# A state-space block and feed-forward on one core: kernel units multiplied by twos, shift added behind the move, gate row spread by DMA, another order

## The chip, the cores and the metric

The kernel runs on one core of one Trainium2 chip. The core has five engines that run beside each other and wait for one another by semaphores: TensorE (PE in the profile, with its weight loads shown as PEld), VectorE (DVE), ScalarE (ACT), GpSimd (POOL) and SyncE (SP), which here issues nearly all DMAs. The metric is the device time of one execution in microseconds; lower is better.

## The reference

All numbers are float32, the sequence has L = 2048 positions, the width is D = 512, the state has N = 128 entries per channel, and the feed-forward is F = 1792 wide.

```
mod = silu(c) @ w_mod                      # six rows of 512: sa, ca, ga, sb, cb, gb
h = layernorm(x) * (1 + ca) + sa
K[d, l] = Re sum_n C[d,n] * exp(dt[d] * A[d,n] * l) * dt[d] * B[d,n]
y = causal convolution of h with K along l  (the reference does it by FFT of length 2 L)
x = x + ga * (y + h * Dskip)
h = layernorm(x) * (1 + cb) + sb
x = x + gb * (relu(h @ w1 + b1)**2 @ w2 + b2)
```

## The kernel before

The convolution is a hand-made transform of the rows in two steps: `stage1` (L784) and `stage2` (L793), each made of small TensorE products, for the input (`u_pieces`, eight blocks c of 64 channels, letters A to H) and for the convolution kernel K. A product in frequency (`product_pieces`, letters a to h: L949 on DVE, then L957 on PE, L963 on DVE) and the inverse (`inverse`, L1131) follow. Then the second normalization and the feed-forward (from L1245 on, some 280 us, mostly products by split float32r parts).

The head (`row_pieces`, L727 to 748) takes the 16 rows of the input, 128 positions by 512 channels each. For every row DVE subtracts the mean and multiplies by a gain row (L729), ACT makes a scaled selection matrix (L737), and PE moves the row into another layout: first a product `pick` x `shift` (L739), which opens the accumulation with the additive part (the shift row s4, made from the modulation group S), and then 32 small products (L742) that add to it. ACT copies the sum from PSUM to `xj` (L745). The gain row needs the modulation groups G and C, the shift needs S as well. Modulation groups are products of PE with 1 MB slabs of `w_mod` (L698).

The string `LOADS` gives the order of the first loads on SP: p and P are the two halves of the state's parameters, x a row of the input, G, C, S the slabs, t the 2 MB table of `stage2`, k and e small tables.

The convolution kernel K is generated in 32 units of 16 channels. For a unit u POOL adds phases (`kgen_phase`, L892) and multiplies amplitudes (`kgen_amp`, L914 and L918) into one of three buffers (`amps[u % 3]`); ACT makes sine and cosine (L902 to 904) into PSUM; DVE multiplies both (`kgen_rl`, L928 to 931); PE multiplies the unit's two halves with each other (`kgen_mm`, L938: 32 products of 32 columns, 64 records since float32 takes two passes) into one half of the bank `kg`; ACT copies it, DVE adds the skip weight (L1018, L1019), and `stage1` takes it on. `finish(u)` (L1010) does all that from the product on.

The string `ORDER` says, for each unit, which other pieces stand behind it in the program (r rows, x exponentials, p parameters, letters for blocks, w loads of w1, l late modulation). That order gives the buffers and the dependencies. The order on each engine is then made by `keep_order` (L181), a list scheduler with its own costs (`weight`, L121): it runs the program forward and backward in turns (`PASSES`), and neighbouring PE instructions that write the same tensor stay together as one group. SP takes what is ready in the order of the program. Instructions named in `in_turn` keep their relative order on PE. Loads after the head go through `paced_load` (L668), at most two in flight.

Around the change of phase, the gate row gb (L762, four rows of 32 equal copies in `gb4`) is spread over all partitions into `gbb` by four products with a broadcast column of the identity and an ACT copy (L1067 to 1071). `gbb` lies in the tile `lo`, which the phases use up to the last unit. The first two calls of `inverse` (rows 0 to 3) add the untouched input, loaded again into `cs_` by the loop at L1089, and their products are put into `in_turn`.

## Time and profile before

| | us |
|---|---|
| median of three runs | 605.31 |
| lowest and highest of them | 601.77, 606.57 |
| profiled execution, its own time | 605.23 |
| span of the profiled execution | 603.4 |

| engine | busy us | share of the span | instructions |
|---|---|---|---|
| PE | 569.5 | 94% | 9396 |
| PEld | 494.1 | 82% | 9396 |
| DVE | 438.4 | 73% | 714 |
| ACT | 421.5 | 70% | 788 |
| POOL | 464.0 | 77% | 383 |

The page gives a profile of one execution. A row of a timeline has start and duration in us, the engine, the line of the code, the operation, the tiles written and read, the shape and how many instructions were merged, and in brackets how long the engine stood idle before it and what ended that wait. Shares are means over stages with different limits, so each part of the change has to be read in its own stage.

### The profile page before, as it was taken

How to read it: one execution, taken by the hardware profiler on the slowest of the kernel's cores; microseconds unless marked ns; L12 is line 12 of the kernel's file. 1: busy time of each engine (PE TensorE's matmuls, PEld its weight loads, DVE VectorE, ACT ScalarE, POOL GpSimd, SP SyncE). 2: the span in 40 equal slices, each digit the busy share in tenths (PEclk: the TensorE clock that was granted, in tenths of full speed). 3: DMA queues.
4: the chain of work that ended last, by engine and by line, in shares of the span. 5: the costliest groups of instructions: out<-in, count | busy, mean ns of one | idle time of the engine just before them, and what ended most of it. 6: DMA issues, size and time to landing. Idle time of an engine off the chain costs nothing.

```text
span 603.4 us, 21634 instructions
## 1 busy us (share of the span) xinstructions
PE 569.5 (94%) x9396; PEld 494.1 (82%) x9396; DVE 438.4 (73%) x714; ACT 421.5 (70%) x788; POOL 464.0 (77%) x383
## 2 busy tenths in 40 slices
PE   1898999999999999998989999999999999998996
PEld 1667988999999998997778888888887888887885
DVE  7796688899798799746888945459859744547833
ACT  4997999998999879442879555546957555654440
POOL 5599999999999799160668998926689688892544
PEclk9999999999999999998999999999999999999999
DMA  8962033302130234274351332015354343201432
GB/s 306 398 193 72 5 73 74 64 12 44 34 74 4 51 104 100 52 195 145 103 147 57 105 104 89 22 45 176 107 153 127 112 119 102 70 18 35 158 88 86
DMA packets 45982, 60.70 MB, mean 101 GB/s; under 512 B 5184, under 2 KB 26816, under 8 KB 45760
## 3 DMA queue, kind: packets, MB, share of 16 engines
q1 hardware_dynamic: 45456, 59.20, 33.5%
q8 instruction: 73, 1.20, 0.9%
q10 hardware_dynamic: 432, 0.14, 0.1%
q14 instruction: 21, 0.17, 0.1%
HBM read 46.74 MB, written 4.19 MB: 84 GB/s over the span
## 4 chain that ended last, share of the span: by engine, by line
PE 69%; ACT 8%; POOL 7%; DVE 6%; issue 5%; DMA 4%; DVEq 0%; POOLq 0%; ACTq 0%; SPq 0%
PE ac L1245 9%; PE ps L1245 8%; PE ps L957 8%; PE ps L799 8%; PE ps L789 6%; PE ac L1274 4%; PE ac L1272 4%; PE ac L1273 4%; PE kg L938 4%; DMA xy<-w 4%; PE kg L1245 3%; PE ac L1131 3%; PE ps L1274 2%; PE ps L1272 2%; PE ps L1273 2%
## 5 line engine op out<-in xcount | busy, mean ns | idle before, releaser
L1214 POOL TENSOR_TENSOR w2r<-xy,w2r 128x512 fp32r<-128x512 f32 x56 | 80.1, 1431 | 53.9 <-ACT w2r L1213 53.7
L799 PE MATMUL ps<-xy,t_sb 128*64 128x64 f32 x2048 | 67.3, 223 | 1.0 <-issue 0.7
L799 PEld LDWEIGHTS ps<-xy,t_sb 128*64 128x64 f32 x2048 | 64.2, 138 | 3.1 <-issue 0.9
L957 PE MATMUL ps<-e_sb,xy 128*64 128x128 f32 (+2 forms) x1152 | 65.3, 267 | 1.1 <-issue 0.8
L957 PEld LDWEIGHTS ps<-e_sb,xy 128*64 128x64 f32 x1152 | 59.5, 140 | 2.6 <-issue 1.4
L1213 ACT CAST w2r<-xy 128x512 fp32r<-128x512 f32 x56 | 34.8, 624 | 27.1 <-PE ac L1274 12.7
L918 POOL TENSOR_TENSOR rtl<-tables 128x1024 f32<-128x1024 f32 x22 | 43.2, 1964 | 0.0
L1272 PE MATMUL ac<-w2r,r 128*128 128x512 f32 x110 | 42.8, 389 | 0.0
L1273 PE MATMUL ac<-w2r,r 128*128 128x512 f32 x110 | 42.8, 389 | 0.0
L1274 PE MATMUL ac<-w2r,r 128*128 128x512 f32 x110 | 42.8, 389 | 0.0
L791 ACT COPY xy<-ps 128x512 f32<-128x512 f32 x64 | 36.6, 590 | 8.7 <-PE ps L789 8.4
L1245 PE MATMUL ac<-tt,k1t 128*128 128x512 f32 x168 | 40.6, 390 | 1.5 <-DVE xy L1378 1.5
L949 DVE TENSOR_TENSOR xy<-ps,xy 128x512 f32<-128x512 f32 x64 | 40.1, 685 | 2.1 <-PE ps L799 1.1
L1245 PEld LDWEIGHTS ac<-tt,k1t 128*128 128x128 f32 x168 | 31.5, 188 | 8.4 <-DVE xy L1378 1.9
L1145 POOL TENSOR_TENSOR big<-big,xy 128x512 f32<-128x512 f32 x12 | 16.1, 1357 | 26.3 <-ACT big L1142 26.2
L1237 POOL TENSOR_TENSOR k1t<-xy,k1t 128x1024 fp32r<-128x1024 f32 x14 | 33.7, 2407 | 3.3 <-ACT k1t L1235 3.1
L892 POOL TENSOR_TENSOR rtl<-lo,big 128x1024 int32<-128x1024 int32 x16 | 34.3, 2143 | 2.4 <-ACT tg L904 2.3
L963 DVE COPY big<-ps 128x256 f32<-128x256 f32 (+1 forms) x66 | 24.7, 411 | 15.7 <-PE ps L957 15.5
L892 POOL TENSOR_TENSOR llph<-lo,big 128x1024 int32<-128x1024 int32 x16 | 34.5, 2157 | 0.8 <-ACT tg L904 0.8
L1272 PE MATMUL ps<-w2r,r 128*128 128x512 f32 (+1 forms) x88 | 34.7, 394 | 0.0
L789 PE MATMUL ps<-d_sb,big 128*64 128x128 f32 x512 | 32.1, 274 | 2.4 <-ACT xy L791 1.7
L1274 PE MATMUL ps<-w2r,r 128*128 128x512 f32 (+1 forms) x88 | 34.0, 386 | 0.0
(297 smaller groups left out, 1693.8 us busy)
## 6 DMA issues: line engine op xcount, KB each, us to landing
xy<-w SPq DMA_DIRECT2D x91, 256.0 KB, 2.8
xy<-xt SPq DMA_DIRECT2D x32, 256.0 KB, 4.5
xy<-xy SPq DMA_DIRECT2D x32, 256.0 KB, 3.6
xy<-w_mod SPq DMA_DIRECT2D x6, 1024.0 KB, 9.0
out_dram<-p SPq DMA_DIRECT2D x15, 256.0 KB, 2.0
t_sb<-c_t SPq DMA_DIRECT2D x1, 2048.0 KB, 11.5
i2c<-c_i SPq DMA_DIRECT2D x4, 512.0 KB, 4.2
big<-prm SPq DMA_DIRECT2D x2, 768.0 KB, 6.2
```

The source lines that it names most:

```text
L789: nc.tensor.matmul(ps[64 * r : 64 * r + 64, 128 * i : 128 * i + 128], src[:, i], d1_sb[:, r], start=True, stop=True)
L791: copy(dst[:, o // 4], ps.rearrange("p (t m) -> p m t", t=4))
L799: nc.tensor.matmul(ps[64 * r : 64 * r + 64, 64 * i : 64 * i + 64].rearrange("p (h q t) -> p q h t", h=2, t=2), t2_sb[:, 8 * g + i, r], src ...
L892: nc.gpsimd.tensor_tensor(ph.rearrange("p d r (a b) -> p (d r) a b", a=4), bc(low_phase[:, us].rearrange("p d r b -> p (d r) b"), 2, 4), b ...
L918: nc.gpsimd.tensor_mul(am[:, 0, :, 32:96].rearrange("p d (v x) -> p d v x", v=2), bc(et[:, 256 + 8 * d0 : 384 + 8 * d0].rearrange("p (y a) ...
L949: nc.vector.tensor_mul(product_piece(y, g), ps, piece(x, g))
L957: nc.tensor.matmul(ps[64 * m : 64 * m + 64], pairs(y)[:, g, i // 2, 64 * m : 64 * m + 64, i % 2], e1_sb[:, h].rearrange("p (r j) -> p r j" ...
L1214: nc.gpsimd.tensor_sub(to[:, 1], wst, to[:, 0].bitcast(F32))
L1245: nc.tensor.matmul(ps[:, cols], x, y, start=(i == 0 and not onto), stop=(i == 5), skip_group_check=onto)
L1272: pe.append(nc.tensor.matmul(bank_, r2l[:, ms], hi_[:, cols], start=(f == begin), stop=False))
L1273: pe.append(nc.tensor.matmul(bank_, r2h[:, ms], lo_[:, cols], start=False, stop=False))
L1274: pe.append(nc.tensor.matmul(bank_, r2h[:, ms], hi_[:, cols], start=False, stop=(f == end_)))
```

## The change

1. `PAIRS`: the products of two neighbouring units are issued one behind the other (`finish_pair`), and the rest of both units follows. One pair of the 16, units 8 and 9, stays apart.
2. `EVAC`: nine of the 16 rows (g, v) have no product with `pick`. For v (five rows) DVE adds the shift while it moves the row out of PSUM, in place of ACT's copy; for g (four rows) ACT copies as before and POOL adds the shift in place. The seven rows a stay as they were.
3. The gate row is spread by 16 DMAs on SP, from 32 partitions to 32 partitions of 128 numbers each, in place of four products and a copy.
4. Four input rows are loaded into `p1` by a piece y, behind the last unit's amplitudes, and the first inverse adds these; the later rows use `ds_` alone.
5. The products of the first two inverse calls are no longer held in their turn on PE.
6. `LOADS`, `ORDER`, `PASSES` (7 to 11) and the scheduler's cost of a transpose are changed, and so the order on every engine.

```
-LOADS = "pxxxxxxxxGCSxxxxxxxkPtxe"
+PAIRS = "1111011111111111"
+EVAC = "gggvaaaaagavvavv"
+LOADS = "xxxpxxxGCxexPSxtxxxxkxxx"
...
-PASSES, SPAN = 7, 400
+PASSES, SPAN = 11, 400
...
 ORDER = (
-    "rrrrrrrrrrxxrrrrrrBCCBpACCBCBAABCCBAB.AAAAC..lB.0aaaa1.a.Daa.x.DabbbbDEDEE.b.2Ebb.bD.DcDccccEDc.E.Fc"
-    "3EFc.E.ddddGd.Fd.GxFd4.F.dGeeeeF..FGGFHeGeGe5..wHeffGHfff.w.f.H.HffH6ggHgw.g.g.H.g7ghhhghw"
+    "rrrrrrrrrrrrrrrrCBCCBAxAAACBlBCCBxAC.p.AACBA.0.BBaaaa1..aDaDa.D.abbbbEE.Db..bEE2bD.bDDcEccDc3..EccxE"
+    ".cFE.cFddFddGdFddF.4.d..eeFee..GGGGFF5xe..eeGeffHwHfGfGfHHfw..H..6HHffggHgg...g.ygw7hwhhhgg"
...
+            if ins.is_transpose:
+                return 88, 88 + 130
...
-            nc.tensor.matmul(ps.rearrange("p (g d) -> p g d", g=4), pick, bc(shift, 1, 4), start=True, stop=False)
+            late = EVAC[s] != "a"
+            if not late:
+                nc.tensor.matmul(ps.rearrange("p (g d) -> p g d", g=4), pick, bc(shift, 1, 4), start=True, stop=False)
...
-                        row[:, 128 * q : 128 * q + 128], start=False, stop=(g == 3))
-            moved.append(nc.scalar.copy(xj[:, :, 4 * s : 4 * s + 4], ps.rearrange("p (g d) -> p d g", g=4)))
+                        row[:, 128 * q : 128 * q + 128], start=late, stop=late or g == 3)
+            to, of = xj[:, :, 4 * s : 4 * s + 4], ps.rearrange("p (g d) -> p d g", g=4)
+            if EVAC[s] == "v":
+                nc.vector.tensor_add(to, of, bc(s4, 2, 4))
+            else:
+                nc.scalar.copy(to, of)
+            if EVAC[s] == "g":
+                nc.gpsimd.tensor_add(to, to, bc(s4, 2, 4))
...
+    def finish_pair(u):
+        if u % 2:
+            for x in (u - 1, u):
+                if x in kq:
+                    kgen_mm(kq.pop(x), kg[:, x % 2])
+            for x in (u - 1, u):
+                if x > finished[-1]:
+                    finish(x)
+        elif PAIRS[u // 2] == "0":
+            kgen_mm(kq.pop(u), kg[:, 0])
+            finish(u)
...
-        kgen_mm(kq.pop(u), kps)
...
+    def early_rows():
+        assert amped[-1] == NU - 1
+        late.append(held(kp, "k01", "p1", [P, 7, 512]))
+        for s in range(4):
+            paced_load(late[0][:, 3 + s], xt[s])
+        yield
...
-            finish(u - 1)
+            finish_pair(u - 1)
...
-    gps = bank("ps", PS)
     for q in range(4):
-        nc.tensor.matmul(
-            gps[:, 128 * q : 128 * q + 128], ident[:, 32 * q : 32 * q + 1].to_broadcast([P, P]), gb4, start=True, stop=True)
-    nc.scalar.copy(gbb, gps)
+        for k in range(4):
+            nc.sync.dma_start(
+                gbb[32 * k : 32 * k + 32, 128 * q : 128 * q + 128], gb4[32 * q : 32 * q + 32])
...
-    xts = [cs_[s] if s < 4 else ds_[s % 4] for s in range(16)]
-    for s in range(8):
+    xts = [ds_[s % 4] for s in range(16)]
+    for s in range(4, 8):
         paced_load(xts[s], xt[s])
...
-    cd4 = runs(spectra[3]).rearrange("p (s q c d) -> p s q c d", s=4, q=4, c=NC)
+    cd4 = p1[:, 3:7].rearrange("p s (q c d) -> p s q c d", q=4, c=NC)
...
-        if s0 < 4:
-            in_turn.update(whole)
```

More of the change, by code (lines that the diff above doesn't have):

```diff
@@ L743, in row_pieces @@
                         ps[32 * q : 32 * q + 32, 128 * g : 128 * g + 128], sel[:, g // 2, 32 * (g % 2) : 32 * (g % 2) + 32],
-                        row[:, 128 * q : 128 * q + 128], start=False, stop=(g == 3))
-            moved.append(nc.scalar.copy(xj[:, :, 4 * s : 4 * s + 4], ps.rearrange("p (g d) -> p d g", g=4)))
+                        row[:, 128 * q : 128 * q + 128], start=late, stop=late or g == 3)
[6 more added lines that the diff above has]
+                nc.gpsimd.tensor_add(to, to, bc(s4, 2, 4))
+            moved.append(s)
             if s % 4 == 3:
@@ L1032, in load_pieces @@
             yield
-    work["w"] = load_pieces()
+    late = []
+    def early_rows():
[4 more added lines that the diff above has]
+        yield
+    work["w"], work["y"] = load_pieces(), early_rows()
     next(work["x"])
@@ L1094, in tile_adaln_ssm_ffn @@
     w2r = held(kp, "k00", "w2r", [P, 3, 2, 512], FR)
-    p1 = held(kp, "k01", "p1", [P, 7, 512])
+    p1 = late[0]
     for _ in last:
```

## The prediction

> **What bounds the kernel now.** I read the page's parts first, then busy times by stage, then the timeline of each engine in the first 56 us, then the waits of POOL, and last single products in the middle.
>
> ```profile
> core 0: us, PE busy (x) PEld busy (x) DVE busy (x) ACT busy (x) POOL busy (x), PEclk, DMA share, GB/s
> 0.00:24.60 24.60, 9.86 (x112) 7.98 (x112) 17.14 (x61) 16.11 (x68) 15.43 (x32) 1.00 0.92 336
> 24.60:49.00 24.40, 23.22 (x528) 16.01 (x528) 23.80 (x48) 23.16 (x65) 19.31 (x26) 1.00 0.62 217
> 49.00:265.00 216.00, 209.97 (x6084) 199.77 (x6086) 177.58 (x290) 188.96 (x293) 196.29 (x144) 1.00 0.26 59
> 320.00:603.40 283.40, 276.93 (x1240) 228.63 (x1238) 179.34 (x217) 161.19 (x279) 209.83 (x167) 1.00 0.31 93
> ```
>
> The rows are stretches of the span, each with the busy time of every engine. Until 24.6 us PE works 9.86 us, because parameters and modulation weights are still arriving. The row stage (24.6 to 49) has PE, DVE and ACT all above 23 of 24.4 us: three engines bind at once. From 49 to 265 PE is busy 210 of 216 us and POOL 196. After 320 PE is busy 277 of 283 us and the diff touches nothing that it does there, so whatever is saved ahead of 320 should come through whole.
>
> **Row stage.** Its start and its pace on PE:
>
> ```profile
> xy<-xt SPq DMA_DIRECT2D x32, 256.0 KB, 4.5
> xy<-w_mod SPq DMA_DIRECT2D x6, 1024.0 KB, 9.0
> big<-prm SPq DMA_DIRECT2D x2, 768.0 KB, 6.2
> 20.38 1.93 PE L698 MATMUL ps<-xy,srep 128*32 128x128 f32 x32 [0.86 <-DMA xy<-w_mod]
> 26.08 1.08 PE L742 MATMUL ps<-xy,big 128*32 128x128 f32 x32 [0.98 <-DVE xy L729]
> 27.09 0.49 PE L739 MATMUL ps<-shift,pick 128*128 128x512 f32 x1
> 27.52 1.08 PE L742 MATMUL ps<-xy,big 128*32 128x128 f32 x32
> 37.86 2.72 DVE L729 SCALAR_TENSOR_TENSOR xy<-xy,mv,kg 128x512 f32<-128x512 f32 x4
> 49.51 2.84 PE L789 MATMUL ps<-d_sb,big 128*64 128x128 f32 x48 [0.70 <-ACT big L745]
> L745 ACT COPY big<-ps 128x512 f32<-128x512 f32 x16 | 9.3, 587 | 1.1 <-PE ps L742 1.0
> L949 DVE TENSOR_TENSOR xy<-ps,xy 128x512 f32<-128x512 f32 x64 | 40.1, 685 | 2.1 <-PE ps L799 1.1
> L1145 POOL TENSOR_TENSOR big<-big,xy 128x512 f32<-128x512 f32 x12 | 16.1, 1357 | 26.3 <-ACT big L1142 26.2
> POOL big L592 <- DMA big<-prm: 5.5, 1, 5.5
> ```
>
> A shift product takes PE's slot from 27.09 to 27.52, 0.43 us, and the 32 products of a row 1.01. Nine rows lose the shift product: 9 x 0.43 = 3.9 us of PE. The first four rows (g, g, g, v) need it no more, so a row waits for the gate and the scale weights (G and C) alone and no longer for the third group S at 20.38 to 22.3. Six rows instead of eight now lie ahead of G and C: 0.5 MB less, at the 336 GB/s of the first window 1.5 us. S was the 1 MB behind C, 3 us more at that rate. Without both, and with the same steps behind, the first row comes 4.5 us earlier, at about 21.6 instead of 26.08. Four such rows fill PE until 25.6. Row 4 is the first with a shift product, and S now has the second parameter load ahead of it, 0.75 MB or 2.3 us; the first shift product ended the wait at 24.6, so row 4 begins at 26.9, and five rows of 1.01 and seven of 1.44 end at 42.0 instead of 48.6. So for PE alone the stage would end 6.6 us earlier. DVE and ACT don't allow that. ACT loses five copies, 5 x 0.587 = 2.9 us, and was busy 23.16 of 24.4. DVE gains five additions out of PSUM; the nearest row is L949's 0.685, so +3.4 us. The last L729 ended at 40.58; with no earlier start, 3.4 us of additions, a row's products (1.08) and one addition more (0.69) let the next stage (L789) begin at 45.8 instead of 49.5, a gain of 3.7; with DVE's start 4.5 us earlier it would be 8.2. Ends 2.9 (ACT) and 6.6 (PE). I take 4.5, nearer the low end, because ACT and DVE were both full. Four rows get an addition in place on POOL; nearest row L1145 with 1.36, 5.4 us in all. What covers them is POOL's 5.5 us wait for the second parameter load. This load now has eight rows ahead of it instead of 15, and two weight groups instead of three: 2.75 MB less, 8 us at 336 GB/s, so the cover is partly eaten by the very gain; POOL's first unit can still start earlier, or at worst as before. The first parameter load goes behind three rows, 2.2 us; POOL's first product on it (L592) waits for the step sizes of L586 anyway: I take nothing, at most 2.2 lost. Rows 9 to 15 now lie behind the table t, but what lies ahead of the last row is the same set of loads: nothing.
>
> **Products by twos.** PE has to change from 64-column to 32-column tiles and back for each unit (L938):
>
> ```profile
> 67.85 1.10 PE L799 MATMUL ps<-xy,t_sb 128*64 128x64 f32 x32
> 68.78 1.04 PE L789 MATMUL ps<-d_sb,ksb 128*64 128x128 f32 x16
> 69.66 1.10 PE L799 MATMUL ps<-xy,t_sb 128*64 128x64 f32 x32
> 70.69 1.12 PE L938 MATMUL kg<-rtl 128*32 128x64 f32 x64
> 71.74 3.02 PE L799 MATMUL ps<-xy,t_sb 128*64 128x64 f32 x96
> 74.69 1.12 PE L938 MATMUL kg<-llph 128*32 128x64 f32 x64
> 92.16 0.97 PE L938 MATMUL kg<-llph 128*32 128x64 f32 x52
> 93.78 0.43 PE L938 MATMUL kg<-llph 128*32 128x64 f32 x12 [0.65 <-issue]
> ```
>
> Thirty-two L799 take 0.93 us ahead of L789 (67.85 to 68.78) and 1.03 ahead of L938. The 96 behind it take 2.95, 0.16 above three times 0.93, of which 0.10 belongs to the next change: 0.05 for the change back. Inside a unit the broken block gives (0.97 - 0.43) / 40 = 13.5 ns per record, so 64 need 0.86, and the unit took 1.05: another 0.19. A unit costs 0.15 to 0.34 us for its changes, and 15 of the 16 pairs lose one such set: 2.3 to 5.1 us of PE.
>
> Against it stands a wait. There are three amplitude buffers, and POOL (L914) writes unit u+2's into that of u-1. With pairs the product of u-1 waits for DVE's L931 of u, so POOL may go on only some 2.2 us (two units' products) behind the end of that L931:
>
> ```profile
> 77.95 1.21 DVE L931 TENSOR_TENSOR rtl<-rtl,tg 128x1024 f32<-128x1024 f32 x1
> 80.14 1.10 POOL L914 TENSOR_TENSOR llph<-tables 128x512 f32<-128x512 f32 x1
> 206.09 1.21 DVE L931 TENSOR_TENSOR llph<-llph,tg 128x1024 f32<-128x1024 f32 x1
> 202.78 1.07 POOL L914 TENSOR_TENSOR rtl<-tables 128x512 f32<-128x512 f32 x1 [0.83 <-PE kg L938]
> 228.60 1.22 DVE L931 TENSOR_TENSOR rtl<-rtl,tg 128x1024 f32<-128x1024 f32 x1
> 230.15 1.07 POOL L914 TENSOR_TENSOR llph<-tables 128x512 f32<-128x512 f32 x1
> 241.26 1.95 POOL L918 TENSOR_TENSOR rtl<-tables 128x1024 f32<-128x1024 f32 x1
> 254.96 1.12 PE L938 MATMUL kg<-rtl 128*32 128x64 f32 x64
> 240.52 1.03 ACT L902 ACTIVATE tg<-llph 128x1024 f32<-128x1024 int32 x1
> ```
>
> The first two rows are units 3 and 5: POOL began at 80.14 and would have to wait until 79.16 + 2.2 = 81.4, so 1.2 us. In the middle pair it is 6.7, in the last 1.9. Over the 14 pairs kept together that have a unit u+2, five would make POOL wait, together 12.2 us at the dates of before; for the other nine the buffer is free anyway. Behind the waiting L914 on POOL stand L918 and the next phase (L892), and ACT's sines and DVE wait for these. POOL has room: its last amplitude ends at 243.2 and the last unit's product runs at 254.96, 11.8 us later. Three ACT passes like L902's (3.1) and DVE's two long and two short ones (2 x 1.21 and 2 x 0.685, 3.8) take 6.9 of these. So 4.9 us of POOL's delay cost nothing, and the new order can draw DVE's work forward. Net of this I take 3.5 of the 5.1, with ends +5.1 and -7.3 (12.2 less 4.9).
>
> **Gate row.** Removed: four products (eight records) and a copy.
>
> ```profile
> 266.01 1.16 PE L1069 MATMUL ps<-gb,ident 128*128 128x128 f32 x8
> 267.48 5.38 PE L957 MATMUL ps<-e_sb,xy 128*64 128x32 f32 x160 [0.30 <-DVE xy L949]
> 240.29 0.35 SPq L1318 DMA_DIRECT2D lo<-b  x1
> 253.06 4.68 SPq L669 DMA_DIRECT2D xy<-xy  x4
> ```
>
> PE gains 267.18 - 266.01, 1.1 us (nothing, if it then waits for DVE all the same). Sixteen moves of 16 KB come onto SP. Their place is free once the last phase is made, about where the load of b2 is issued, 240.29; an issue takes 0.35, 16 make 5.6 us, and the next thing on SP is the swap at 253.06: 12.8 us of cover. If one cost more than 0.8 us the swap, and with it the last block's products, would be late by the rest. I take nothing.
>
> **Early rows, inverse out of turn, transposes' weight, passes.** Four loads move off the stretch from 270 on. The first sum of the inverse waited there for PE and not for a load: nothing. The freer order of the first inverse can move single waits; bounds -1 to +1.5, I take nothing.
>
> **Sum.** 4.5 + 3.5 + 1.1 = 9.1 us. The profiled execution took 605.23 us (span 603.4 and 1.8 around it), the median of the runs is 605.31, the same within 0.1. So 605.2 - 9.1 = 596.1, say 596.
>
> [...] The group of L698 at 20.38 takes 1.93 us for 32 records:
>
> ```profile
> 78.78 1.95 PE L698 MATMUL ps<-xy,srep 128*32 128x128 f32 x64
> ```
>
> In the middle 64 of them take 1.95: in the head PE runs at half pace, although the row of that window gives a granted clock of 1.00; from L742 at 26.08 on the pace is full. A row stage that begins sooner, behind less work, could begin at the half pace. If its first four rows do, they take 8.1 us instead of 4 and end at 29.7 instead of waiting for 26.9: 2.8 us of the gain are lost, 598.8. I give it a small chance, since DVE feeds a row every 0.69 us and PE should be dense at once. [...]
>
> **Rivals.** (1) All comes out: head 6.6, pairs 5.1, gate 1.1 give 592.4, with the inverse 590.9. For: PE is the bound nearly everywhere. Against: ACT and DVE in the row stage. (2) The waits eat the pairs, or ACT holds the head: head 2.9, pairs 0 to -2, gate 0 to 1.1 give 601 to 604, no change that counts. For: ACT at 23.16 of 24.4. This is also the case in which the edits do not do what they say. (3) Slower: POOL becomes the bound. If the amplitude buffer's wait stays 12.2 us and POOL starts no earlier, because its four additions fill the 5.5 us, its last amplitude ends at 255.4 and the last unit's product at 262.3 instead of 254.96: 7.3 later, 612.5 (the gate's 1.1 being lost in DVE's wait). It decides once POOL's delay passes 4.9 us plus what its start gains. Against: the five waits are mostly a question of the place of DVE's work.
>
> **Chances.** A measurement of this kernel can tell about 1%, 6.05 us, from no change. Forecast 0.47 (own range 592 to 599), slow clock at the start 0.07, all comes out 0.13: faster 0.67. Rival 2 has 0.24, rival 3 has 0.09. The range 590 to 605 leaves out rival 3, a little of rival 2 and little more, 0.15 to 0.2 together.
>
> **What would show it.** The first L742 near 21.6 us and the first L789 near 45; L739 seven times; L938 in blocks of 128; POOL's waits for PE kg under 5 us in the sum; no L1069; SP free again before the last swap. Wrong would be: the first L789 at 48 or later, or POOL's last L918 later than 243.

## The result and the profile after

The changed kernel takes 613.15 us in the median of four runs (612.24 to 614.34), the kernel before 604.65 beside it (601.77 to 606.57): 1.0145 times as long, interval 1.0113 to 1.0176. The forecast was 596.0, range 590 to 605. The profiled execution of the changed kernel took 614.34 us, span 612.5.

Where the time goes can be read from the starts of a few groups on TensorE. Line numbers of the changed kernel lie further down: L653 became L657, L742 L748, L739 L745, L745 L755, L789 L802, L914 and L918 L927 and L931, L938 L951, L1131 L1163, L1272 L1302. The row move of VectorE is L753, GpSimd's row addition L757.

| us from the start of the span | before | after | difference |
|---|---|---|---|
| first product of a row (L742, L748) | 26.08 | 22.60 | -3.5 |
| first product of stage 1 (L789, L802) | 49.51 | 50.00 | +0.5 |
| end of the last unit's products (L938, L951) | 256.08 | 261.60 | +5.5 |
| first product of the inverse (L1131, L1163) | 272.79 | 281.05 | +8.3 |
| first product of the second feed-forward matrix (L1272, L1302) | 320.15 | 328.64 | +8.5 |
| end of the span | 603.4 | 612.5 | +9.1 |

So rows begin sooner, but the stage behind them does not, and then 8 us are lost up to the inverse. The busy times by stretch of after, for the stretches that the prediction showed of before (columns as there, then TensorE's granted clock, DMA share and GB/s):

```profile
24.60:49.00 24.40, 19.64 (x519) 15.06 (x511) 22.61 (x46) 22.79 (x64) 23.93 (x28) 0.98 0.74 252
49.00:265.00 216.00, 202.03 (x5858) 191.18 (x5860) 184.28 (x285) 179.07 (x286) 189.35 (x139) 0.98 0.23 53
```

In the row stage TensorE has 3.6 us less to do than before (19.64 for 23.22) and GpSimd 4.6 more (23.93 for 19.31). From 49 to 265 every engine but VectorE is busy for less time than in before: something makes them stand. Among the groups of VectorE, ScalarE and GpSimd, VectorE's integer shifts are the only one whose longest member jumped, from 0.95 to 7.81 us. The group of that line in before and then in after (shortest, median, longest ns):

```profile
L653 DVE TENSOR_SCALAR big<-big x10: 283/675/951, 14.3 to 120.9; 128x512 int32<-128x512 int32 x6, 128x256 int32<-128x256 int32 x4
```

```profile
L657 DVE TENSOR_SCALAR big<-big x10: 292/802/7814, 12.5 to 137.5; 128x512 int32<-128x512 int32 x6, 128x256 int32<-128x256 int32 x4
```

VectorE's timeline of after around the longest one:

```profile
101.19 1.22 DVE L942 TENSOR_TENSOR llph<-llph,tg 128x1024 f32<-128x1024 f32 x1
102.32 7.81 DVE L657 TENSOR_SCALAR big<-big 128x512 int32<-128x512 int32 x1
110.06 0.67 DVE L943 TENSOR_TENSOR llph<-llph,tg 128x512 f32<-128x512 f32 x1
110.66 0.15 DVE L1042 TENSOR_TENSOR ksb<-kg,ds 128x4 f32<-128x4 f32 x1
...
116.70 0.42 DVE L657 TENSOR_SCALAR big<-big 128x512 int32<-128x512 int32 x1
```

The shift of the same shape at 116.70 takes 0.42 us, this one 7.81. GpSimd's timeline meanwhile:

```profile
101.83 1.07 POOL L927 TENSOR_TENSOR rtl<-tables 128x512 f32<-128x512 f32 x1
102.86 1.96 POOL L931 TENSOR_TENSOR rtl<-tables 128x1024 f32<-128x1024 f32 x1
104.77 2.15 POOL L905 TENSOR_TENSOR rtl<-lo,big 128x1024 int32<-128x1024 int32 x1
106.86 1.08 POOL L927 TENSOR_TENSOR rtl<-tables 128x512 f32<-128x512 f32 x1
107.89 1.97 POOL L931 TENSOR_TENSOR rtl<-tables 128x1024 f32<-128x1024 f32 x1
113.95 2.13 POOL L905 TENSOR_TENSOR llph<-lo,big 128x1024 int32<-128x1024 int32 x1 [4.10 <-ACT tg L917]
```

Five products follow one another without a gap, and the shift ends (110.13) when the fifth does (109.86) and GpSimd has to wait for ScalarE. What stands behind the shift on VectorE is small, but others wait for it. The timelines of ScalarE and of TensorE in after, and the busy times of the stretch behind:

```profile
110.84 0.37 ACT L1041 COPY ksb<-kg 128x256 f32<-128x256 f32 x1 [6.01 <-DVE ksb L1042]
```

```profile
111.52 1.98 PE L802 MATMUL ps<-d_sb,big 128*64 128x128 f32 x16 [5.14 <-DVE big L976]
113.28 3.63 PE L802 MATMUL ps<-d_sb,ksb 128*64 128x128 f32 x32
```

```profile
110.00:130.00 20.00, 18.48 (x426) 17.96 (x428) 17.98 (x32) 16.58 (x28) 12.94 (x10) 0.83 0.23 49
```

ScalarE stands 6.01 us, TensorE 5.14, and then TensorE runs at half pace: 16 of these products take 1.98 us (the prediction's row has 1.04), 32 take 3.63, and the granted clock of the stretch is 0.83. GpSimd then stands 4.10 us too, because the sines that it waits for were late. On TensorE alone that is 5.14 us of standing and, against the pace of the prediction's row, some 2.5 us of half pace ((1.98 - 1.04) + (3.63 - 2.08)), 7.6 in all from one 0.4 us instruction. The experiments had to show whether this is so, and why the change gains nothing even beside it.

### The profile page after: what moved, and what is told of

The parts are those of the page before. It is cut to its first block, busy times and chain, and to the rows that moved or that the text cites. A ratio compares the mean times of both kernels' runs of the same rounds, so it can differ in the third digit from the quotient of the medians.

```text
span 612.5 us, 21636 instructions
## 1 busy us (share of the span) xinstructions
PE 565.7 (92%) x9379; PEld 493.0 (80%) x9379; DVE 450.5 (74%) x719; ACT 415.1 (68%) x780; POOL 467.5 (76%) x387
## 4 chain that ended last, share of the span: by engine, by line
PE 66%; DVE 13%; POOL 10%; ACT 5%; issue 4%; DMA 1%; SPq 0%; DVEq 0%; POOLq 0%; ACTq 0%
PE ac L1275 9%; PE ps L1275 7%; PE ps L970 6%; PE ps L802 5%; PE ps L812 5%; PE ac L1302 4%; PE ac L1303 4%; PE ac L1304 4%; PE ps L1304 3%; PE ps L1303 3%; PE ps L1302 3%; PE kg L1275 3%; DVE xy L962 3%; PE kg L951 2%; PE ac L1163 2%
## 5 line engine op out<-in xcount | busy, mean ns | idle before, releaser
L970 PE MATMUL ps<-e_sb,xy 128*64 128x128 f32 (+2 forms) x1152 | 63.9, 266 | 1.6 <-issue 1.0
L804 ACT COPY xy<-ps 128x512 f32<-128x512 f32 x64 | 36.9, 594 | 11.0 <-PE ps L802 10.9
L931 POOL TENSOR_TENSOR rtl<-tables 128x1024 f32<-128x1024 f32 x22 | 43.3, 1970 | 0.0
L1302 PE MATMUL ac<-w2r,r 128*128 128x512 f32 x110 | 42.8, 389 | 0.0
L962 DVE TENSOR_TENSOR xy<-ps,xy 128x512 f32<-128x512 f32 x64 | 40.0, 685 | 1.7 <-PE ps L812 1.1
L802 PE MATMUL ps<-d_sb,big 128*64 128x128 f32 x512 | 33.2, 280 | 8.5 <-DVE big L976 5.1
L802 PEld LDWEIGHTS ps<-d_sb,big 128*64 128x64 f32 x512 | 28.8, 139 | 10.9 <-DVE big L976 5.4
L802 PE MATMUL ps<-d_sb,ksb 128*64 128x128 f32 x512 | 34.9, 284 | 1.2 <-issue 0.7
```

The source lines that it names most:

```text
L802: nc.tensor.matmul(ps[64 * r : 64 * r + 64, 128 * i : 128 * i + 128], src[:, i], d1_sb[:, r], start=True, stop=True)
L804: copy(dst[:, o // 4], ps.rearrange("p (t m) -> p m t", t=4))
L931: nc.gpsimd.tensor_mul(am[:, 0, :, 32:96].rearrange("p d (v x) -> p d v x", v=2), bc(et[:, 256 + 8 * d0 : 384 + 8 * d0].rearrange("p (y a) ...
L962: nc.vector.tensor_mul(product_piece(y, g), ps, piece(x, g))
L970: nc.tensor.matmul(ps[64 * m : 64 * m + 64], pairs(y)[:, g, i // 2, 64 * m : 64 * m + 64, i % 2], e1_sb[:, h].rearrange("p (r j) -> p r j" ...
L1302: pe.append(nc.tensor.matmul(bank_, r2l[:, ms], hi_[:, cols], start=(f == begin), stop=False))
```

## The experiments

In the kernels below that are called "the order of after" or "of before", the order that `keep_order` had made on every engine was written down and held, so that only the edit differs. Times are medians; the ratio is to runs of before on the same chip.

| kernel | us | ratio to before, interval |
|---|---|---|
| inc_on_pool | 605.22 | 1.0025, 1.0007 to 1.0043 |
| inc_later | 604.86 | 1.0027, 1.0007 to 1.0047 |
| shift_first | 604.37 | 0.9997, 0.9975 to 1.0020 |
| shift_again | 609.55 | 1.0092, 1.0063 to 1.0121 |
| pairs_alone | 617.49 | 1.0239, 1.0209 to 1.0269 |
| pool_less | 604.65 | 1.0027, 1.0009 to 1.0045 |
| pool_relief | 612.77 | 1.0167, 1.0106 to 1.0228 |
| before_relief | 608.81 | 1.0081, 1.0045 to 1.0116 |
| pe_more | 613.16 | 1.0170, 1.0134 to 1.0205 |
| pe_less | 607.97 | 1.0053, 1.0023 to 1.0084 |
| before_pe_less | 607.01 | 1.0038, 1.0017 to 1.0059 |
| act_less | 606.15 | 1.0050, 1.0022 to 1.0077 |
| pe_pool_less | 604.69 | 1.0022, 0.9991 to 1.0053 |
| all_less | 605.41 | 1.0021, 0.9988 to 1.0053 |
| head_dve_less | 604.88 | 1.0010, 0.9986 to 1.0035 |
| rows_sooner | 607.20 | 1.0052, 1.0026 to 1.0078 |
| loads_less | 604.10 | 0.9983, 0.9962 to 1.0005 |
| loads_and_work_less | 605.75 | 1.0003, 0.9980 to 1.0025 |

### The long shift

**inc_on_pool.** The order of after; the shift by one of the second parameter half becomes an addition on GpSimd. Theory A, here and in the expectations of inc_later and shift_again, is that VectorE waits there for GpSimd and that this wait costs the time (604 to 606 us for this kernel).

```
-        shift(inc, p1, 1)
+        iadd(inc, p1, p1) if c0 else shift(inc, p1, 1)
```

> The changed kernel with its order kept instruction by instruction; only the one shift that took DVE 7.81 us at 102.32 (the increment of the second parameter half, L657) is made by POOL as an addition of the number to itself, at the same place of the order. [...] Rival B (the pairs and the wait for amplitude buffers cost the time, POOL being the bound): 611 to 614, since POOL has 1.3 us more to do.

**inc_later.** The order of after with one place changed; the same shift stays on VectorE, behind the next shift of that line (`h1`) instead of in the middle of a unit's products. Nothing in the code above the written order changes.

```
 VectorE:
-  shift(inc, p1, 1); rest of this unit's products, the next unit's; shift(h1, p1, 3)
+  rest of this unit's products, the next unit's; shift(h1, p1, 3); shift(inc, p1, 1)
```

> The changed kernel with its order kept; only the same shift stands 13 places later on DVE, right behind the next shift of its kind (which took 0.42 us at 116.70). Theory A: 604 to 607, if the shift finds a gap of POOL there; if it is caught again the time stays near 613 and the long row moves with it. Rival B: 612 to 614, with no long row.

Both gave back about 8 us: 605.22 and 604.86 for 613.15. They also showed that the next shift inherits a part of it (VectorE's timeline of inc_on_pool):

```profile
109.69 3.32 DVE L657 TENSOR_SCALAR big<-big 128x512 int32<-128x512 int32 x1
```

That is the remaining shift, 3.32 us instead of 0.42; it starts at 109.69 us. By an estimate GpSimd is then again in a row of products: in after the row ended at 109.86 us, and here it holds one addition more (those of this shape take 1.28 us in after), which makes some 111 us. In inc_later the two shifts at this place took 3.10 us together. By the times of both kernels this cost little.

**shift_first.** The order of after to the last instruction, with one wait more: GpSimd's second product of those five (102.86 us) waits for the shift. It says whether the gapless row of products is the cause.

```
-    for x, y in behind:
+    for x, y in [*behind, (groups[360][0], groups[554][0])]:
```

> The order of after, exactly, with one wait more: GpSimd's second amplitude product at 102.86 us (the instruction behind the one during which the long shift was issued) waits for that shift. If the 7.81 us come from GpSimd's products following each other without a gap, the shift now takes 0.9 to 1.5 us, since only one product can be under way, ScalarE's 6.0 us and TensorE's 5.1 us of waiting and its half pace behind them go, and the time is 604 to 606.5. Rival (the shift is slow for another reason, or the loss of after sits elsewhere in its order): the shift stays over 3 us, or the time stays at 611 to 614.

The time fell to 604.37. VectorE's and GpSimd's timelines of shift_first:

```profile
101.73 1.05 DVE L657 TENSOR_SCALAR big<-big 128x512 int32<-128x512 int32 x1
102.70 0.68 DVE L943 TENSOR_TENSOR llph<-llph,tg 128x512 f32<-128x512 f32 x1
```

```profile
102.86 1.96 POOL L931 TENSOR_TENSOR rtl<-tables 128x1024 f32<-128x1024 f32 x1 [0.37 <-DVE big L657]
```

The shift now waits for the one product under way and then runs, 1.05 us in all; VectorE goes on at 102.70 instead of 110.06, and GpSimd gives up 0.37 us for it. With this the cause of the 8.8 us between after and shift_first is shown three ways: the instruction on another engine, at another time, and in its place with a gap for it.

**shift_again.** The order of before, with that shift repeated eight times, each behind a unit's products (units 7 to 14).

```
-        shift(inc, p1, 1)
+        for _ in range(9 if c0 else 1):
+            shift(inc, p1, 1)
```

> The kernel before with its order kept and eight more shifts of the same kind (the same numbers written again, 128x512 int32), one behind L929 of each of the units 7 to 14, where POOL works without a pause. Theory A: their durations differ, most between 0.4 and 2.5 us (one POOL instruction to wait for), some several POOL instructions long; the time grows by several us, 608 to 620. Rival C (the 7.81 us was something of that one run and place): all take 0.4 to 1.3 us, and the time grows by at most 3 us, since DVE has some slack.

In its profile the nine took 0.42 to 1.12 us each: where before's order puts them, a shift gets in behind the product that is under way. One of them, and GpSimd's products beside it:

```profile
104.92 1.12 DVE L653 TENSOR_SCALAR big<-big 128x512 int32<-128x512 int32 x1
```

```profile
104.70 1.06 POOL L915 TENSOR_TENSOR rtl<-tables 128x512 f32<-128x512 f32 x1
105.73 2.13 POOL L919 TENSOR_TENSOR rtl<-tables 128x1024 f32<-128x1024 f32 x1
107.83 2.14 POOL L893 TENSOR_TENSOR rtl<-lo,big 128x1024 int32<-128x1024 int32 x1
```

Yet the time was 609.55 and scattered (605.83 to 612.55, the profiled execution at 606.38). Whether a shift was caught in the longer executions no profile shows, so this run is inconclusive on the price. It shows that meeting GpSimd's products does not by itself make a shift long, not even where they follow one another without a gap, as here. What decides whether a shift gets in behind the first of them or is passed over stays open; a gap in front of the second (shift_first) let it in.

**pool_relief.** Made for another question (below): the order of inc_later, with seven amplitude products (L927) on VectorE instead of GpSimd. It met the same collision with another operation. VectorE's timeline of pool_relief, and one row of GpSimd's:

```profile
101.70 6.66 DVE L927 TENSOR_TENSOR rtl<-tables 128x512 f32<-128x512 f32 x1
...
161.41 0.68 DVE L927 TENSOR_TENSOR llph<-tables 128x512 f32<-128x512 f32 x1
```

```profile
112.17 2.14 POOL L905 TENSOR_TENSOR llph<-lo,big 128x1024 int32<-128x1024 int32 x1 [4.36 <-ACT tg L917]
```

A float product with both operands in SBUF takes 6.66 us in the stretch where the shift took 7.81, and 0.68 to 2.31 in the six other units; GpSimd then waits 4.36 us for ScalarE, and the time is 612.77. VectorE's products with an operand in PSUM (L942, 1.22 us in the list of after) ran beside GpSimd's products at their usual length: all 32 of after take 1.207 to 1.225 us. What sets them apart from the shift and the float product, no run here shows. How long such a wait lasts the runs do show: the shift was passed over by four more instructions of the other engine, and the float product, which starts beside the GpSimd product of 100.83 us and ends at 108.36, by three (102.74 to 107.81).

### What the pairs do by themselves

**pairs_alone.** Before with `PAIRS` and `finish_pair` only; the scheduler makes its own order.

> The kernel before with the products by twos as the only edit (its ORDER string and LOADS kept, the planner orders anew). Theory A (pairs are harmless): 600 to 604, PE saves 2 to 5 us. Rival B (the buffer's wait makes POOL the bound): 608 to 614, with POOL's waits for PE kg and for ACT above 8 us.

617.49, the slowest of all, and inconclusive: the scheduler's new order also made the head later. GpSimd's first phase came at 53.47 us instead of 48.97 and its last amplitude at 258.07 instead of 243.21, with no shift over 1.53 us. An edit to one piece changes the place of all others here, and that was worth more than the edit. In all the other kernels of this list the order was therefore held.

### Who bounds the stage of the units

With the long shift mended the changed kernel still takes 604.4 to 605.2 us, though TensorE has some microseconds less to do. The first theory was that GpSimd had become the bound.

**pool_less, pool_relief, before_relief.** In seven units (u = 5, 9, ... 29) the first amplitude product is made for one sixteenth (pool_less), or on VectorE in the order of inc_later (pool_relief) and of before (before_relief).

```
-        nc.gpsimd.tensor_mul(
-            am[:, 0, :, 0:32].rearrange("p d (a b) -> p d a b", a=4),
+        n = 1 if u > 4 and u % 4 == 1 else 16; nc.gpsimd.tensor_mul(
+            am[:, 0, 0:n, 0:32].rearrange("p d (a b) -> p d a b", a=4),
...
-        nc.gpsimd.tensor_mul(
+        (nc.vector if u > 4 and u % 4 == 1 else nc.gpsimd).tensor_mul(
```

> The order of inc_later (604.86 us, 1.0027 of before), but the first amplitude product of seven units (5, 9, ... 29; 512 columns, 1.07 us on GpSimd) is made for one sixteenth of its columns only, so those units keep old values in the rest. GpSimd gets some 6.6 us less to do between 44 and 244 us, nothing else changes. Theory P (without the long shift GpSimd is what bounds the stage of the units, and that is where the savings on TensorE went): its last amplitude ends 4 to 6.6 us earlier, near 238, and the time is 599 to 601. Rival Q (TensorE still bounds, and the new order itself costs what the change saves): 604 to 605.5, with GpSimd waiting longer. Rival R (ScalarE, 182 of 215 us there, sets the pace): 604 to 605.5, with GpSimd's waits for ACT longer by the saved 6 us.

> As pool_less, but VectorE makes these seven products in full (all columns, the output is the reference's). GpSimd loses 7 x 1.07 = 7.5 us, VectorE gets about 7 x 0.7 = 4.9 us on top of 182 of 215 us. Theory P: 599 to 602, faster than before and after. Rival Q: 604.5 to 606. Rival R (the work only moves, VectorE is late for ScalarE's copies or stands at a buffer): 605 to 609.

> The order of before, with the first amplitude product of the same seven units on VectorE: 7.5 us less on GpSimd, no part of the change in it. Theory P, if GpSimd bounds before as well: 598 to 601. If before is bound by TensorE there (210 of 216 us busy), as the prediction has it: 602.5 to 604.5. VectorE in the way: over 605.

That theory fell: 604.65 with 5.5 us less on GpSimd (its groups of L927 take 28.7 us instead of 34.2). The two kernels that give the work to VectorE lose, pool_relief by the collision above and before_relief with three of its seven products at 2.15 to 2.41 us instead of 0.69.

**pe_more, pe_less, before_pe_less.** The opposite theory is the prediction's own, that TensorE bounds. Six units' products made twice, or seven units' products made for one quarter, the latter in both orders.

```
-                    kgen_mm(kq.pop(x), kg[:, x % 2])
+                    am = kq.pop(x); [kgen_mm(am, kg[:, x % 2]) for _ in range(2 if x in (5, 9, 13, 17, 21, 25) else 1)]
...
-                    kgen_mm(kq.pop(x), kg[:, x % 2])
+                    kgen_mm(kq.pop(x), kg[:, x % 2], 1 if x > 4 and x % 4 == 1 else 4)
```

> The order of inc_later, but the kernel-unit products of six units (5, 9, 13, 17, 21, 25) are made twice in the same place, with the same result: 6 x 1.0 = 6 us more on TensorE between 44 and 244 us. Theory P (TensorE has slack there, GpSimd bounds): 605 to 607. Rival Q (TensorE bounds): 609.5 to 611, the whole 6 us.

> The order of inc_later, with the kernel-unit products of seven units (5, 9, ... 29) made for one quarter only (the other three quarters keep old values): 7 x 0.78 = 5.5 us less on TensorE. pe_more lost 8.5 us for 6 us more. Theory T (TensorE's work is what the stage lasts by): 598.5 to 601. Rival W (in this order the other engines' chain is as long as TensorE's, so more work on it costs and less does not pay): 603.5 to 605.5, with TensorE idle 5 us more.

> The same omission in the order of before. This is the prediction's own premise, that a microsecond saved on TensorE between 49 and 265 us is a microsecond of time: 597 to 599. Rival W: 602 to 604, the whole saving turns into waiting, in before as in after.

More work on TensorE costs more than itself: 8.3 us (613.16 for 604.86), though from the first stage 1 to the last unit's product TensorE is busy only 5.1 us longer (200.9 for 195.8). The rest is standing, most of it for nothing that the profile names (7.3 us of such waits there, 3.1 in inc_later). And less work gains nothing. Its busy time in the same stretch fell by 4.5 us in pe_less (191.2 for 195.8) and by 4.3 in the order of before (196.8 for 201.1), somewhat less than the 5.5 expected, and the times were 607.97 and 607.01. The stage itself became 0.6 us shorter in either order (table below). So TensorE is not a bound in the sense of the prediction, not before and not after. That both kernels came out slower, not equal, no run explains; in the profile of before_pe_less stage 1 already began 2.6 us later than in before, though its head is the same.

**act_less, pe_pool_less, all_less.** ScalarE alone (the cosine of the seven units for a quarter), TensorE and GpSimd together, and all three.

```
-        last_sin[0] = nc.scalar.activation(flat_(cs), flat_(ab), AF.Sin, scale=-TWO_PI / TURN, bias=halfpi)
+        n = 256 if sins.append(0) or len(sins) > 5 and len(sins) % 4 == 2 else 1024; last_sin[0] = nc.scalar.activation(flat_(cs)[:, 0:n], flat_(ab)[:, 0:n], AF.Sin, scale=-TWO_PI / TURN, bias=halfpi)
```

> The order of inc_later, with the cosine pass of the same seven units made for a quarter of its columns (the rest keeps what the bank held): 7 x 0.8 = 5.5 us less on ScalarE, nothing else. Theory V: 603 to 605.5, as with the other two engines. Rival S (ScalarE is the single bound of the stage, 182 of 215 us busy but always late for somebody): 598.5 to 601.

> The order of inc_later with both omissions of pe_less and pool_less at once: 5.5 us less on TensorE and 6 us less on GpSimd, in the same seven units. Each alone gave nothing (stage 0.6 and 0.35 us shorter). Theory V (the units go round a loop GpSimd, ScalarE, VectorE, TensorE with two or three buffers, all four near full, so shortening one engine only makes it wait for the others): still 603 to 605.5, because ScalarE and VectorE are as before; the stage from the first stage 1 to the inverse 222 to 223.5 us. Rival U (TensorE and GpSimd are the two that hold each other): 599 to 601.5, the stage 218 to 220.

> The order of inc_later with the three omissions together: 5.5 us less on TensorE, 6 on GpSimd, 5.5 on ScalarE, VectorE as before. Theory V: now something comes out, 598.5 to 602, since three of the four in the loop are shorter. If the time still stays at 603 to 605.5, the fixed order with VectorE holds the stage, or its savings come out as waiting behind it, between the last unit and the inverse.

None is faster than before. The stretches, worked out from the first and last rows of TensorE in each profile, say where savings end (units: first stage 1 to the last unit's product; tail: to the inverse; inverse: to the second feed-forward matrix). In brackets is TensorE's idle time that no other engine ends, which the profile calls issue.

| profile | units | tail | inverse (issue) |
|---|---|---|---|
| before | 206.6 | 16.7 | 47.4 (4.3) |
| after | 211.6 | 19.5 | 47.6 (2.5) |
| shift_first | 203.6 | 19.5 | 45.9 (4.1) |
| inc_later | 204.4 | 19.5 | 45.3 (3.5) |
| pool_less | 203.8 | 19.7 | 46.1 (2.4) |
| pe_less | 203.8 | 19.5 | 48.1 (5.1) |
| act_less | 205.0 | 19.5 | 44.2 (1.9) |
| pe_pool_less | 200.8 | 19.5 | 48.7 (6.0) |
| all_less | 202.1 | 21.1 | 47.6 (4.7) |
| before_pe_less | 206.0 | 16.7 | 49.0 (5.0) |
| pe_more | 212.5 | 19.5 | 45.8 (2.5) |

Against inc_later, less on one engine shortens the units by 0.6 us or not at all; on two, by 3.6; on three, by 2.3. These are single profiles, and shift_first, which leaves nothing out, differs from inc_later by 0.8. So none of TensorE, GpSimd and ScalarE bounds the stage alone. No run takes work from VectorE there, so that VectorE does is a rival that stands: in pe_less TensorE waits 4.3 us for its products L962 instead of 1.7, and 2.4 for ScalarE's copies L804 instead of 1.4. The reading that fits all runs, argued and not isolated, is that the units go round from GpSimd over ScalarE and VectorE to TensorE with two or three buffers; in inc_later these are busy 195, 183, 183 and 207 of the 216 us from 49 to 265. And what is saved there is then lost behind it, mostly in the inverse. TensorE's timeline of pe_pool_less, whose inverse begins 3.7 us before that of inc_later (273.49):

```profile
269.83 1.90 PE L1163 MATMUL ac<-big,i2c 32*32 32x128 f32 x128
...
282.89 1.33 PE L1163 MATMUL ac<-big,i2c 32*32 32x128 f32 x78 [1.33 <-issue]
...
299.75 0.26 PE L1163 MATMUL ac<-big,i2c 32*32 32x128 f32 x1 [1.64 <-issue]
...
318.53 0.39 PE L1302 MATMUL ac<-w2r,r 128*128 128x512 f32 x1
```

At 299.75 one last product of such a block stands alone, and TensorE stands 1.64 us before it, for nothing that the profile names. Its second feed-forward matrix starts at 318.53, at 318.84 in inc_later.

**loads_less, loads_and_work_less.** Is TensorE there waiting for its own instructions, because loads of data hold these up? From 274 to 312 us of inc_later the two queues that carry instructions moved 0.17 MB, the queue of the data 4.49 MB. Twelve loads of input rows between 274 and 308 us are cut to an eighth, on top of inc_later and of pe_pool_less.

```
-        paced_load(xts[s], xt[s])
+        paced_load(xts[s][:, 0:64], xt[s][:, 0:64])
...
-                    paced_load(xts[s + 4], xt[s + 4])
+                    paced_load(xts[s + 4][:, 0:64], xt[s + 4][:, 0:64])
```

> The order of inc_later, with the twelve loads of whole rows for the residual (256 KB each, issued between 274 and 308 us) cut to an eighth (64 of 512 columns; those rows' residual is then wrong in the rest). No engine but SyncE's queue gets less work. Theory C: in the inverse's stretch TensorE waits for its own instructions (idle with no releaser, 3.5 of 4.4 us in inc_later), because their loading competes with these 3 MB; the waits there fall under 1.5 us and the time to 601 to 603.5. Rival D (the waits come with the place of the code and not with the loads): 603.5 to 605.5, the same waits.

> The same cut on top of pe_pool_less, whose inverse began 3.7 us earlier (269.8 instead of 273.5) and whose TensorE then stood 6.0 us with no releaser in the inverse's stretch (48.7 us long instead of 45.3). Theory C: the stretch falls to 43 to 46 us and the saved work comes out, 597 to 601. Rival D: 603.5 to 605.

604.10 and 605.75: it is not these loads. With the DMA share from 275 to 319 us at 0.24 instead of 0.43, TensorE still stood 3.7 us with no releaser in loads_less (3.5 in inc_later). The last run also shows how far one profile reaches: its work up to 270 us is that of pe_pool_less, and the units took 202.2 us, the tail 21.1, instead of 200.8 and 19.5. What these waits are stays open, and with it why savings ahead of the inverse don't come out.

### The head

**head_dve_less.** The order of inc_later, row normalizations for a quarter of the columns.

```
-            nc.vector.scalar_tensor_tensor(row, row, mv1[:, s, 0:1], g1, op0=ALU.subtract, op1=ALU.mult)
+            nc.vector.scalar_tensor_tensor(row[:, 0:128], row[:, 0:128], mv1[:, s, 0:1], g1[:, 0:128], op0=ALU.subtract, op1=ALU.mult)
```

> The order of inc_later, with the 16 row normalizations (0.734 us each on VectorE, 25.6 of 27.4 us busy in the row stage) made for 128 of 512 columns (the rest of a row stays as it came): some 7.5 us less on VectorE, the rows' products and moves as they were. If VectorE ends the row stage: the first product of stage 1 at 44 to 47 us instead of 49.6, and if a gain ahead of the stage of the units comes out, 600 to 602. If ScalarE ends it (25.7 of 27.4): the first product of stage 1 at 48 to 49.6 and the time 603.5 to 605.5. A start that is 3 us earlier with a time that does not move would say that GpSimd and ScalarE, which start the units at 43.9 whatever the rows do, set the pace behind it.

The busy times from 22 to 50 us, of inc_later and then of head_dve_less:

```profile
22.00:50.00 28.00, 22.79 (x559) 18.55 (x561) 26.15 (x55) 26.32 (x71) 27.53 (x32) 0.90 0.74 260
```

```profile
22.00:50.00 28.00, 21.05 (x566) 16.70 (x560) 19.78 (x52) 26.57 (x72) 27.53 (x32) 1.00 0.75 260
```

VectorE (third busy time) has 6.4 us less to do, and the first product of stage 1 comes at 49.19 instead of 49.60. So it is not these normalizations; VectorE's additions out of PSUM stayed as they were. ScalarE (26.57 of 28) and GpSimd (27.53 of 28) are as full as ever.

**rows_sooner.** The order of inc_later; two blocks of eight exponentials on ScalarE behind the row copies that followed them, and the powers of rows 12 to 15 ahead of an integer product on GpSimd.

```
 ScalarE:
-  8 exponentials; row copies and scalings of rows 7 to 9
+  row copies and scalings of rows 7 to 9; 8 exponentials
 GpSimd:
-  integer product; powers of rows 12 to 15
+  powers of rows 12 to 15; integer product
```

> The order of inc_later with three steps of the row stage exchanged, all work kept: ScalarE's two blocks of eight exponentials (2.0 us each at 35.4 and 42.3 us) go behind the row copies that stood behind them, and GpSimd makes the powers for rows 12 to 15 (1.24 us) ahead of a 1.28 us integer product. If ScalarE's and GpSimd's order is what kept the row stage from its expected gain, TensorE's waits for ScalarE there (0.9, 0.9, 1.3 us) shrink and the first product of stage 1 comes at 47 to 48.6 instead of 49.6. By the loop of theory V the time then gains nothing to 1 us: 603.5 to 605; if the head's gains come out whole: 602 to 603.5. If the rows' end is unchanged at 49.3 to 50, the order there was not what held it.

It went the wrong way: stage 1 began at 50.76, the time is 607.20. The exponentials had been filling a gap, since ScalarE now stood 2.28 us for the moments of the rows (L686), and the last row copy came behind the exponentials and the sine's table. So this change of the order of ScalarE and GpSimd takes no slack.

## Why the prediction was wrong

**The collision: not in the sum.** The step that failed most is the one on "early rows, inverse out of turn, transposes' weight, passes", whose only price for a new order was "single waits; bounds -1 to +1.5, I take nothing". The new order put one VectorE instruction against an unbroken row of GpSimd's, and that costs 8 to 9 us (613.15 against 604.37 to 605.22). Among the shifts of before nothing shows it: the longest took 0.951 us. But the same collision stands in the feed-forward of before, on a subtraction of VectorE with both operands in SBUF. Its group, its longest member, and GpSimd's instructions beside that:

```profile
L1405 DVE TENSOR_TENSOR r<-rs,r x12: 678/1365/3370, 404.6 to 567.6; 128x512 fp32r<-128x512 f32 x12
```

```profile
543.28 3.37 DVE L1405 TENSOR_TENSOR r<-rs,r 128x512 fp32r<-128x512 f32 x1
```

```profile
542.25 1.33 POOL L1214 TENSOR_TENSOR w2r<-xy,w2r 128x512 fp32r<-128x512 f32 x1
543.50 2.60 POOL L1372 TENSOR_TENSOR big<-big,lo 128x512 f32<-128x512 f32 x2
```

It took 3.37 us where its shortest took 0.68, and ended when the third GpSimd product did. So a look at the longest members of before would have shown that a new order can cost more than single waits.

**The row stage: 4.5 taken, -0.5 measured.** The first row came at 22.60 instead of the 21.6 forecast, and seven products with `pick` are left, as said. But stage 1 began at 50.00, behind the 48 that was named as a sign of being wrong. (A pair of single profiles is a thin basis for the size: in the three kernels that hold before's order and leave its head alone, stage 1 began at 50.09, 51.31 and 52.09, in those that hold after's at 49.4 to 49.8. So the stage may have gained about 1 us, but not the 2.9 to 6.6 of the working.) Rows of after that bear on it (TensorE's and ScalarE's timelines, and SyncE's waits):

```profile
22.60 1.94 PE L748 MATMUL ps<-xy,big 128*32 128x128 f32 x32 [1.90 <-ACT tg L640]
...
30.88 0.50 PE L745 MATMUL ps<-shift,pick 128*128 128x512 f32 x1 [1.11 <-ACT big L755]
...
50.00 4.59 PE L802 MATMUL ps<-d_sb,big 128*64 128x128 f32 x80 [1.58 <-DVE big L753]
```

```profile
41.61 0.70 ACT L741 ACTIVATE big<-ident,mv 128x128 f32<-128x128 f32 x2 [1.30 <-POOL mv L690]
```

```profile
SPq L552 <- DMA t_sb<-c_t: 4.7, 1, 4.7
```

The half pace at the start, a rival, did occur: 1.94 us for a row's 32 products instead of 1.08. It seems to have cost nothing of the end, because TensorE then waited for ScalarE anyway (1.11 us at 30.88). What the working missed, as far as waits can show it, is how much ScalarE and GpSimd hold the stage. From 24.6 to 49 ScalarE spends 3.1 us less in copies, as forecast, but 1.7 more in table loads, 1.3 more in exponentials and 0.9 in the first unit's sine. GpSimd got four row additions, two of them behind its first phase, which itself came earlier (44.29 for 48.97), and ScalarE waits for its powers (1.30 us). The step "what lies ahead of the last row is the same set of loads: nothing" did not hold either: SyncE waits 4.7 us for the table t ahead of the last three rows, and issues the last of them at 29.09 instead of 22.34. Which of these alone holds the end is not settled; that VectorE's normalizations do not is shown by head_dve_less.

**The pairs: 3.5 taken.** TensorE's groups of unit products, before and then inc_later:

```profile
L938 PE MATMUL kg<-rtl 128*32 128x64 f32 x1408 | 25.8, 221 | 0.9 <-issue 0.9
L938 PE MATMUL kg<-llph 128*32 128x64 f32 x640 | 11.5, 221 | 0.6 <-issue 0.6
```

```profile
L951 PE MATMUL kg<-rtl 128*32 128x64 f32 x1408 | 23.5, 220 | 0.5 <-issue 0.5
L951 PE MATMUL kg<-llph 128*32 128x64 f32 x640 | 11.6, 220 | 0.0
```

By these sums they save 37.3 - 35.1 = 2.2 us, but a pair that reads from both tiles counts in both rows where its two units overlap. From the start of each block to the start of what follows it, waits left out, all units take 35.2 us in before and 32.1 in inc_later: 3.1 us, within the 2.3 to 5.1 of the working. The wait for the amplitude buffers, the doubt of the working, was small: GpSimd stood 3.5 us for `kg` in after, under the 5 named. The stage of the units is 2.2 us shorter, 204.4 for 206.6; whether the pairs did this no run separates. It is gone at the inverse, because the tail behind the last unit is 2.8 us longer (19.5 for 16.7) with TensorE busy throughout: the new order leaves more of its work behind the last unit.

**The gate row: 1.1 taken.** The products are gone, and the sixteen moves held up no swap (seven of them were issued behind the last one). By the premise, the next point, that need not gain anything.

**The premise.** That "whatever is saved ahead of 320 should come through whole" is the step behind all terms, and it is refuted for before itself: before_pe_less, 4.3 us less on TensorE and a ratio of 1.0038. A busy share of 210 in 216 us was read as a bound. Of the 4.3 us the units got 0.6 (206.0 for 206.6); the rest came back as waits of TensorE inside the stage. The stretch behind 320, of which the prediction took no change, did not stay the same either: from the first product of the second feed-forward matrix to the end it lasts 283.8 to 284.3 us in the kernels that hold after's order and 282.7 to 283.3 in before and those that hold its order, for a reason that no run shows.

**The rivals.** The rival for slower named 612.5, very near the result, but by another mechanism (GpSimd as the bound behind the amplitude buffers, its last amplitude at 255.4; it was 250.31, and pool_less speaks against that bound). A right number for a wrong reason. The rival of no change, 601 to 604, comes nearest to the change without its collision: 604.4 to 605.2, ratios 0.9997 to 1.0027.

## What to carry to other kernels

Before a busy engine is priced as the bound, take some of its work away in a held order and see whether the time follows; here 4.3 us less on the busiest engine gained nothing. In a timeline, look at the longest member of each group and not at its mean: one VectorE instruction with its operands in SBUF, behind GpSimd work without gaps, can last several of GpSimd's instructions (7.81 us for 0.42, beside five of them); here one wait that opened a gap of 0.4 us mended it. An order made anew by a scheduler moves the time by more than most edits (pairs_alone), so compare edits in one held order.

## What the runs showed of the hardware

- A 0.42 us shift of VectorE lasted 7.81 us beside five GpSimd products in a row, and a 0.68 us product with both operands in SBUF lasted 6.66 beside four; elsewhere a shift that met GpSimd's products got in behind one (shift_again, up to 1.12 us), and one lasted 3.32 us (inc_on_pool). Products of VectorE with an operand in PSUM kept their length (all 32 of L942 in after 1.207 to 1.225 us).
- After 5.14 us of idling TensorE ran at half pace for some 5 us (16 records of stage 1 in 1.98 us instead of 1.04), which adds some 2.5 us to the wait; the granted clock of the stretch was 0.83.
- A float32 product of TensorE shows as two records (a unit's 32 products, 64 records, 2048 for the 32 units of before), a float32r product as one (the 16 shift products of before, 16 records). Counts read off a timeline are of records: a row's 16 products in the code (L742) are the 32 of its rows.
- From the first product of the inverse to the second feed-forward matrix TensorE stood 1.9 to 6.0 us for nothing that the profile names, most in the profile that came there first (pe_pool_less); with the loads of rows in that stretch cut to an eighth it was 3.7 us for 3.5, so they are not the cause.
